# A mixer block on one core: first block normalised by ln and exp, polynomial sines on GpSimd, w2 in seven-row runs, fewer loads, another stored order

## The chip, the cores and the metric

One core of one Trainium2 chip. The metric is the device time of one execution in microseconds (us). Lower is better. The engines are named as in the profile: PE (TensorE matmuls), PEld (its weight loads), DVE (VectorE), ACT (ScalarE), POOL (GpSimd), SP (SyncE, here only the queue that issues most DMAs).

## The reference, cut to what matters

```python
xn = layernorm(x)                                   # x: [1, 2048, 448], bf16
# branch A: a diagonal complex recurrence of 448 states
Lam_bar = exp(exp(log_dt) * Lam);  B_bar = ((Lam_bar - 1) / Lam)[:, None] * B
h = Lam_bar * h + xn[t] @ B_bar.T                   # for each of 2048 steps t
s = 2 * real(h @ C.T) + xn * Dskip
# branch B: a gated MLP, F = 1792
y = layernorm(xn)
g = silu(gelu(y @ w1 + b1) @ w2 + b2)
out = x + s * g
```

The output is 2048 x 448 in bf16.

## The kernel before, in words

The 2048 rows are cut into four groups of 512 (`g` = 0 to 3), each into two blocks of 256 rows (`b`). A block lies on 128 partitions as two "parities" (`par`): partition p holds rows 2p and 2p+1. The work of a group is:

- `ln_stats`, `ln_scale`, `ln_apply` (lines 484 to 533): mean and variance by DVE, the reciprocal square roots for both layernorms by a chain of small operations, then two normalised copies, `xn_sb` for branch A and `xn2_sb` for branch B. For group 0 `ln_scale` is a chain of eleven dependent DVE operations on [128, 2 or 4] operands (an integer first guess and two Newton steps, lines 505 to 515). For later groups POOL or DVE does it.
- `xt` (line 535): transposes to `xnT` and `xn2T`. For `xn2T` of group 0 PE does them (line 544) and DVE copies the result from PSUM (line 550); all others are DMA transposes on the SP queue.
- `mm1` (line 768) and, for group 0, `mm1_half` (line 782): `w1` as stationary operand, `xn2T` as moving operand of 512 (or 256) columns, then GELU by ACT into `gT`. `mm1_half` does one block at a time, 7 steps of 8 matmuls for each block, into three pairs of PSUM banks in turn, so that the fourth step waits for the first step's GELU.
- `mm2` (line 799): 14 matmuls of `gT` by `w2`, then bias by DVE, tanh by ACT, gate by DVE.
- `bu` (line 703): B·x through `BT`, 14 or 7 matmuls of 256 columns into one PSUM bank, evacuated by ACT into `u_sb`.
- `ssm` (line 721): rotation by tables `WT`, DVE scans, rotation back into `h_sb`.
- `ym` (line 811): C·h plus the skip terms, times the gate, plus x, and the store.

The parameters are made once (`parameters`, line 558): four small vectors are loaded by the ACT queue, turned by PE (lines 561 to 565), and run through about forty operations on [128, 4] columns, nearly all on POOL (lines 572 to 621). The sine and cosine of two angles for each state come from two ACT `Sin` operations (lines 582 and 583). From the result come `lr`, `li` (real and imaginary part of Lam_bar), with which `lb` (line 666) makes a second copy of B, and the `BT` DMA transposes (line 674) follow; `cq` (line 685) makes `CQ` and `CZ` from the transposed C (`Cr`, line 678), and `m0` (line 693) a product of both. `tables` (line 628) makes the rotation tables `WT` by five ACT `Sin` operations after the last GELU of group 0.

PE first runs two batches of dummy matmuls on `ident` (line 858), 20 and 32 of them, with the turning of the parameters between them.

Three sets of ACT functions are in use (number 0 with exp and tanh, 9 with sin, 11 with GELU and tanh); where the next operation needs another set, the built program holds a load instruction for it (`ACT_TABLE_LOAD` in the trace). The program of the kernel before holds six.

The order of the instructions is not that of the text. Every operation is a `Task` with buffers read and written and an assumed duration, latency and priority; `Plan.order` (line 141) schedules them on a model of the five engines, `Plan.search` (line 220) changes priorities at random for 20,000 rounds, and `emit` (line 276) writes the best order out. Each engine runs its instructions strictly in that order and waits on semaphores. So every wait stands in front of all that follows on its engine.

Of the kernel before, what the change touches and what calls it, by code (L numbers as in the profile page):

```python
# [8 lines left out]
ACT = mybir.ActivationFunctionType  # L9
# [5 lines left out]
PINNED = -1e5  # L15

SLACK = 0.13
ENGS = ("pe", "act", "dve", "pool", "sp")

BEGIN, SWAP = 0.8, 1.28  # L20

AHEAD, AHEAD_T = 5.5, 0.9

HEAT = 0.03

DRAIN = 0.1

FULL = (0, 0)


class Task:

    __slots__ = ("eng", "ins", "reads", "writes", "dur", "lat", "prio", "sem", "nbytes", "idx",
                 "deps", "succ", "start", "end", "name", "chain", "alts", "alt", "table", "far", "mode", "move", "hold")

    def __init__(self, eng, ins, reads, writes, dur, lat, prio, sem, nbytes, name):
        self.eng, self.ins, self.reads, self.writes = eng, ins, tuple(reads), tuple(writes)  # L40
        self.dur, self.lat, self.prio, self.sem, self.nbytes = dur, lat, prio, sem, nbytes
        self.name = name
        self.deps, self.succ = set(), []
        self.start = self.end = None
        self.chain = False
        self.table = self.mode = None
        self.far, self.move, self.hold = AHEAD, 0.0, 0.0
        self.alts, self.alt = [(self.eng, self.ins, self.dur, self.lat)], 0

    def choose(self, k):  # L50
        self.alt = k
        self.eng, self.ins, self.dur, self.lat = self.alts[k]
        if self.sem in ENGS:
            self.sem = self.eng


class Plan:
# [3 lines left out]
    GBPS = 285.0  # L61
# [21 lines left out]
    def add(self, eng, ins, reads=(), writes=(), dur=0.2, lat=0.1, prio=0.0, sem=None, nbytes=0, name="",  # L83
            chain=False, table=None):
        if callable(ins):
            ins = [ins]
        t = Task(eng, ins, reads, writes, dur, lat, prio, sem or eng, nbytes, name)
        t.idx = len(self.tasks)
        t.chain = chain
        t.table = table  # L90
        self.tasks.append(t)
        return t

    def either(self, first, second, reads=(), writes=(), prio=0.0, chain=False):

        t = self.add(first[0], first[1], reads, writes, dur=first[2], lat=first[3], prio=prio)
        t.alts.append((second[0], second[1] if isinstance(second[1], list) else [second[1]], second[2], second[3]))
        t.chain = chain
        return t

    def dma(self, eng, out_ap, in_ap, reads=(), writes=(), prio=0.0, nbytes=0, transpose=False, dur=0.45, name="dma"):
        sem = f"d{self.ndma}"
        self.ndma += 1
        self._sem(sem)

        def fn(e):
            if transpose:
                return e.dma_start_transpose(out_ap, in_ap)
            return e.dma_start(out_ap, in_ap)  # L109
        if transpose:  # L110
            dur = 1.3
        if eng == "pool":
            dur = 1.0
        t = self.add(eng, fn, reads, writes, dur=dur, lat=1.4 if transpose else 1.8, prio=prio, sem=sem, nbytes=nbytes, name=name)
        t.far = AHEAD_T if transpose else AHEAD
        t.move = 1.3 * nbytes / 229376 if transpose else nbytes / (self.GBPS * 1e3)
        return t

    def link(self):
# [17 lines left out]
        for t in self.tasks:  # L137
            for d in t.deps:
                d.succ.append(t)

    def order(self):
        left = {t: len(t.deps) for t in self.tasks}
        ready = {e: [] for e in ENGS}
        free = {e: BEGIN for e in ENGS}
        table, mode = None, 0
        dma_free = 0.0
        at = {}
        pick = {e: None for e in ENGS}
        out = []

        def enter(t):
            m = t.hold
            for d in t.deps:
                end = d.end - d.lat + 0.03 if d.sem == t.eng else d.end + 0.03
                if end > m:
                    m = end
            at[t] = m
            ready[t.eng].append(t)

        for t in self.tasks:  # L160
            if not left[t]:
                enter(t)
        stale = set(ENGS)
        while True:
            for e in stale:
                r = ready[e]
                if not r:
                    pick[e] = None
                    continue
                f = free[e]  # L170
                first = min([at[t] for t in r])
                limit = (first if first > f else f) + SLACK
                best = None
                for t in r:
                    if at[t] <= limit and (best is None or t.prio < best.prio or (t.prio == best.prio and t.idx < best.idx)):
                        best = t
                pick[e] = (first if first > f else f, best)
            stale.clear()
            e = None
            for k in ENGS:  # L180
                if pick[k] is not None and (e is None or pick[k][0] < pick[e][0]):
                    e = k
            if e is None:
                break
            t = pick[e][1]
            start = max(at[t], free[e])
            if t.table and t.table != table:
                start = max(at[t], free[e] + SWAP)
                table = t.table
            if e == "pe":  # L190
                if (t.mode or FULL)[0] != mode:
                    start += DRAIN
                mode = (t.mode or FULL)[1]
            t.start = start
            done = start + t.dur
            t.end = done + t.lat
            if t.nbytes:
                if e == "sp":
                    done = max(done, dma_free + t.move - t.far)
                begin = start + (0.2 if t.far == AHEAD_T else t.dur)  # L200
                if t.nbytes > 8192 and begin < dma_free:
                    begin = dma_free
                t.end = begin + t.move + t.lat
                if t.nbytes > 8192:
                    dma_free = t.end - t.lat
            free[e] = done
            ready[e].remove(t)
            stale.add(e)
            for u in t.succ:
                left[u] -= 1  # L210
                if not left[u]:
                    enter(u)
                    stale.add(u.eng)
            out.append(t)
        assert len(out) == len(self.tasks)
        self.total = max(t.end for t in out)
        out.sort(key=lambda t: (t.start, t.idx))
        return out

    def search(self, rounds, seed=1):  # L220


        tail = {}
        for t in reversed(self.tasks):
            tail[t] = t.dur + max([tail[s] + (t.lat if s.eng != t.eng else 0.03) for s in t.succ], default=0)
        given = [t.prio for t in self.tasks]
        both = [i for i, t in enumerate(self.tasks) if len(t.alts) > 1]

        loads = [i for i, t in enumerate(self.tasks) if t.nbytes > 8192 and given[i] > PINNED]

        def run(prios, alts, holds):
            for t, p, a, h in zip(self.tasks, prios, alts, holds):
                t.prio = p
                t.hold = h
                if a != t.alt:
                    t.choose(a)
            self.order()
            return self.total

        alts, holds = [t.alt for t in self.tasks], [t.hold for t in self.tasks]  # L240
        free = [i for i, p in enumerate(given) if p > PINNED]
        now = None
        for alpha in (0.0, 0.1, 0.3, 1.0, 3.0, 1000.0):
            prios = [p - alpha * tail[t] if p > PINNED else p for t, p in zip(self.tasks, given)]
            total = run(prios, alts, holds)
            if now is None or total < now:
                now, here = total, (prios, alts, holds)
        best, keep = now, here
        mean = sum(here[0][i] for i in free) / len(free)
        scale = math.sqrt(sum((here[0][i] - mean) ** 2 for i in free) / len(free))  # L250
        rng = random.Random(seed)
        for r in range(rounds):
            prios, alts, holds = list(here[0]), list(here[1]), list(here[2])
            n = rng.choice((1, 1, 2, 4, 8))
# [7 lines left out]
            elif kind < 0.6:  # L262
                i, d = rng.randrange(len(free)), rng.gauss(0, scale * rng.choice((0.02, 0.1, 0.3)))
                for j in free[i:i + n]:
                    prios[j] += d
# [675 lines left out]
```

## Time and profile before

| | |
|---|---|
| median of 4 runs | 165.27 us (164.82 to 166.33) |
| the profiled execution | 165.44 us, of which 163.70 us are the span of the profile |
| busy, share of the span | PE 96%, DVE 77%, ACT 57%, POOL 17% |
| first `mm1_half` matmul | 10.43 us |
| start of the last matmuls, of the last DVE operation | 160.03 us, 160.79 us |
| one `ACT_TABLE_LOAD` | 1.28 us, six in all |
| matmuls | 993 |

The page gives one profiled execution. Its chain of waits follows the last instruction back to what released each step; the timeline lists the instructions in order of time with the idle time in front of them and what ended it. A matmul's record is longer than the distance to the next one, since matmuls are pipelined; the chain and the distances between the starts tell what a stream of them costs.

### The profile page before, as it was taken

The page shows a single profiled execution, that of the slowest core. Times are in us where ns is not written, and L with a number is a line of the kernel's source. Part 1 is how long each engine was busy: PE and PEld are TensorE (multiplying, and loading weights), DVE is VectorE, ACT ScalarE, POOL GpSimd, SP SyncE. Part 2 cuts the span into 40 slices and gives each one's busy share as a digit, 9 for nine tenths or more (in the row PEclk, how much of TensorE's full clock was granted, in tenths as well). Part 3 has the DMA queues.
Part 4 walks back from the last instruction along what each step waited for, and adds up shares of the span by engine and source line. Part 5 has one row for each costly group of instructions (what it writes and reads, how often), then busy time and mean ns, then how long its engine had stood idle before and what let it go on. Part 6 is the DMA issues. An engine that isn't in the chain of part 4 may idle for free.

```text
span 163.7 us, 2764 instructions
## 1 busy us (share of the span) xinstructions
PE 157.0 (96%) x993; PEld 95.4 (58%) x993; DVE 126.0 (77%) x264; ACT 92.9 (57%) x151; POOL 28.1 (17%) x96
## 2 busy tenths in 40 slices
PE   5979999999999999999999999999999999999991
PEld 5958985656546665554445455666566655555561
DVE  4866999657979989998989973545983699988563
ACT  3756984996868898627729544221449672541100
POOL 5866000700000030000606550000005020000000
PEclk9999999999999999999999999999999999999999
DMA  4999999798777000920000047440201000100111
GB/s 123 275 282 305 334 168 171 146 179 155 165 163 234 0 0 0 72 60 0 0 0 2 4 112 152 93 103 9 56 0 56 0 4 0 56 0 0 60 56 58
DMA packets 32807, 14.95 MB, mean 91 GB/s; under 512 B 25973, under 2 KB 32761, under 8 KB 32794
## 3 DMA queue, kind: packets, MB, share of 16 engines
q1 hardware_dynamic: 32738, 14.66, 40.6%
q0 software_dynamic: 48, 0.11, 0.3%
q8 instruction: 8, 0.13, 0.3%
q14 instruction: 5, 0.04, 0.1%
q10 hardware_dynamic: 8, 0.00, 0.0%
HBM read 7.00 MB, written 1.84 MB: 54 GB/s over the span
## 4 chain that ended last, share of the span: by engine, by line
PE 92%; DVE 2%; ACT 2%; DMA 1%; ACTq 1%; issue 0%
PE psum L803 24%; PE psum L772 22%; PE psum L707 13%; PE psum L824 12%; PE psum L788 9%; PE psum L827 4%; PE psum L696 3%; PE psum L858 2%; DMA vrows<-in_A_Dskip_dram 1%; ACT WT L647 1%; PE psum L544 1%; PE psum L833 1%; DVE t L837 1%; ACTq L109 1%; DVE tmp L839 1%
## 5 line engine op out<-in xcount | busy, mean ns | idle before, releaser
L803 PE MATMUL psum<-w_sb,gT 128*128 128x448 bf16 x224 | 44.7, 352 | 0.0
L772 PE MATMUL psum<-xn2T,w_sb 128*128 128x512 bf16 x168 | 38.7, 379 | 0.1
L803 PEld LDWEIGHTS psum<-w_sb,gT 128*128 128x128 bf16 x224 | 21.7, 98 | 18.6
L779 ACT ACTIVATE gT<-psum 128x1024 bf16<-128x1024 f32 x21 | 21.5, 1024 | 17.5 <-PE psum L772 17.1
L772 PEld LDWEIGHTS psum<-xn2T,w_sb 128*128 128x128 bf16 x168 | 16.2, 98 | 17.6 <-issue 0.3
L707 PE MATMUL psum<-xnT,BT 128*128 128x256 bf16 x196 | 24.0, 272 | 0.3 <-ACT WT L647 0.3
L707 PEld LDWEIGHTS psum<-xnT,BT 128*128 128x128 bf16 x196 | 19.0, 98 | 5.7 <-ACT WT L647 0.7
L807 ACT ACTIVATE th<-o 128x448 f32<-128x448 f32 x16 | 9.1, 575 | 22.8 <-DVE o L806 22.7
L806 DVE TENSOR_TENSOR o<-psum,b2bc 128x448 f32<-128x448 f32 x16 | 9.9, 621 | 9.2 <-PE psum L803 9.2
L788 PE MATMUL psum<-xn2T,w_sb 128*128 128x256 bf16 x112 | 14.4, 294 | 0.8 <-DVE xn2T L550 0.8
L837 DVE TENSOR_TENSOR t<-psum,g_sb 128x448 bf16<-128x448 f32 (+2 forms) x17 | 10.1, 595 | 6.4 <-PE psum L827 4.8
L732 DVE TENSOR_TENSOR_SCAN s_f<-cw,cur,v_sb 128x256 f32<-128x256 f32 x21 | 14.5, 735 | 0.2
L788 PEld LDWEIGHTS psum<-xn2T,w_sb 128*128 128x128 bf16 x112 | 11.7, 105 | 3.3 <-DVE xn2T L550 1.1
L808 DVE SCALAR_TENSOR_TENSOR g_sb<-th,o 128x448 bf16<-128x448 f32 x16 | 9.8, 619 | 3.0 <-ACT th L807 2.8
L824 PE MATMUL psum<-CQ,h_sb 128*128 128x448 bf16 (+2 forms) x63 | 12.0, 332 | 0.0
L824 PE MATMUL psum<-CZ,h_sb 128*128 128x448 bf16 x56 | 11.9, 352 | 0.0
L795 ACT ACTIVATE gT<-psum 128x512 bf16<-128x512 f32 x14 | 8.2, 595 | 6.4 <-PE psum L788 6.1
L746 POOL TENSOR_TENSOR cwk<-s_f,ang 128x3 f32<-128x3 f32 x3 | 1.2, 409 | 58.0 <-DVE s_f L732 58.0
L711 ACT ACTIVATE u_sb<-psum 128x512 bf16<-128x512 f32 x12 | 7.1, 595 | 6.8 <-PE psum L707 6.2
L488 DVE BATCH_NORM_STATS2 lnst<-x_all 128x6 f32<-128x448 bf16 x16 | 9.7, 614 | 1.3 <-DMA x_all<-in_A_x_dram 1.2
L528 DVE TENSOR_SCALAR xn_sb<-x_all,lnw 128x448 bf16<-128x448 bf16 x21 | 7.9, 394 | 2.1 <-ACT xn_sb L529 1.1
L529 ACT ACTIVATE xn_sb<-x_all,lnw 128x448 bf16<-128x448 bf16 x11 | 7.9, 750 | 2.1 <-DVE xn_sb L528 2.1
(130 smaller groups left out, 195.3 us busy)
## 6 DMA issues: line engine op xcount, KB each, us to landing
w_sb<-in_B_w_dram SPq DMA_DIRECT2D x2, 784.0 KB, 10.2
out_dram<-tmp SPq DMA_DIRECT2D x7, 224.0 KB, 1.9
w_sb<-in_B_w_dram SPq DMA_DIRECT2D x2, 672.0 KB, 7.0
x_all<-in_A_x_dram SPq DMA_DIRECT2D x3, 448.0 KB, 5.0
x_all<-in_A_x_dram SPq DMA_DIRECT2D x2, 224.0 KB, 2.7
gT<-in_A_C_re_dram SPq DMA_DIRECT2D x1, 392.0 KB, 9.9
Bn<-in_A_B_re_dram SPq DMA_DIRECT2D x1, 336.0 KB, 8.5
Bn<-in_A_B_im_dram SPq DMA_DIRECT2D x1, 336.0 KB, 8.1
```

The costliest lines, as they stand in the source:

```text
L488: dve([lambda e, b=b, par=par, q=q: e.bn_stats(lnst[:, q, :], x_all[:, 2 * g + b, par, :])], [f"x{2 * g + b}"] + (["xmT0_0"] if (g, b, par ...
L707: fns = [lambda e, r=r, m=m, d=d: e.matmul(psum[:, 4, r * NK:(r + 1) * NK], BT[:, m, d, :], xnT[:, gx, d, :], start=(d == 0), stop=(d == 6 ...
L732: dve(lambda e, i=i, ri=ri, init=init: e.tensor_tensor_scan(s_f[:, i, ri, :], col(R2, i).to_broadcast([128, NK]), v_sb[:, i, ri, :], init, ...
L772: fns = [lambda e, k=k, d=d: e.matmul(psum[:, b0 + k, :], w1_sb[:, d, (2 * j + k) * 128:(2 * j + k + 1) * 128], rhs[:, d, :, :], start=(d ...
L779: act(lambda e: e.activation(gT[:, gb, 2 * j:2 * j + 2, :], psum[:, b0:b0 + 2, :], ACT.Gelu_apprx_tanh), [f"ps{b0}", f"ps{b0 + 1}"] + (WK ...
L788: fns = [lambda e, k=k, d=d: e.matmul(psum[:, banks[k], :].rearrange("p (r c) -> p r c", r=2)[:, :, cs], w1_sb[:, d, (2 * j + k) * 128:(2 ...
L803: fns = [lambda e, fi=fi: e.matmul(psum[:, bk, 0:D], gT[:, gb, fi, q * 128:(q + 1) * 128], w2_sb[:, fi, :], start=(fi == 0), stop=(fi == N ...
L806: dve(lambda e: e.tensor_tensor(o2[:, fb, :], psum[:, bk, 0:D], b2bc[:], ALU.add), [f"ps{bk}", "b2bc"], [f"oo{fb}"], 0.62, prio - 76)
L807: act(lambda e: e.activation(th[:, fb, :], o2[:, fb, :], ACT.Tanh, scale=0.5), [f"oo{fb}"] + (WK + WKP if g == 0 else []), [f"th{fb}"], 0. ...
L808: dve(lambda e: e.scalar_tensor_tensor(out=g_sb[:, gs, :], in0=th[:, fb, :], scalar=1.0, in1=o2[:, fb, :], op0=ALU.add, op1=ALU.mult), [f" ...
L824: fns = [lambda e, k=k: e.matmul(psum[:, bk, c0:c1], h_sb[:, hb, k, k0:k0 + 128], cm[:, k, c0:c1], start=(k == 0), stop=False) for k in ra ...
L837: dve(lambda e: e.tensor_tensor(t3[:, fb, c0:c1], psum[:, bk, c0:c1], g_sb[:, gs, c0:c1], ALU.mult), [f"ps{bk}", f"g{gs}"], [f"t3{fb}_{c0} ...
```

## The change

1. The first block of group 0 is normalised for each parity by itself. DVE takes mean and variance of one parity, ACT makes the reciprocal square root as exp(-0.5 ln(v)), DVE applies it, PE does four transposes and DVE a copy of 512 columns. The load of this block of x is in two halves. The scale of the branch-A copy of that block comes from a third Ln and Exp, and two POOL operations. Block 1 stays on the DVE chain. The first ACT operation, a warm-up, is Ln in place of Exp.
2. The two ACT `Sin` of the parameters are replaced by a polynomial on POOL: three operations to wrap the angle, one ACT `Abs`, ten POOL operations in a chain.
3. `w2` is loaded so that each partition reads seven neighbouring rows in one piece (7 x 448 elements); hidden feature 7p+t of a half then lies on partition p, and `w1`'s columns are taken with a step of seven elements (`fcol`) as the stationary operand of `mm1` and `mm1_half`.
4. Two loads of B (64 x 448 each) and two of C (112 x 4 x 64 each) are left out. The swapped copies that they made are replaced by taking the two halves of the partitions crosswise in `combine`, two operations of 64 partitions in place of one of 128, for the last tile of each of B, CQ and CZ.
5. The load of block 1 of x is moved behind the first half of `w1`. The dummy matmuls are 28 and 8. The eight `De` and `Do` operations are made after the third GELU step.
6. The planner is taken out; a stored order takes its place, with `SECOND`, a list of the operations that go to their other engine.

```diff
-            act(lambda e: e.activation(sgn[0:1, 3:4], sgn[0:1, 2:3], ACT.Exp), ["sgn"], ["warm"], 0.2, S0, "exp")
+            act(lambda e: e.activation(sgn[0:1, 3:4], sgn[0:1, 2:3], ACT.Ln, scale=-1.0), ["sgn"], ["warm"], 0.2, 4 * PINNED, "exp")
...
-            ldx(0, 1, S1)
-            ldx(1, 1, S1)
+            for par in range(2):
+                ld("sp", x_all[:, 0, par, :], dram_ap(A_x, par * D, [[2 * D, 128], [1, D]]), [f"x0p{par}"], 114688, S1)
             ldw1(0, S1 + 1)
+            ldx(1, 1, S1 + 2)
...
-                for k, m in ((ri, 6), (1 - ri, 7)):
-                    ld("sp", Bn[k * 64:k * 64 + 64, m, D:896], dram_ap(bm, 384 * D, [[D, 64], [1, D]]),
-                       [f"Bn{m}{ri}"], 57000, S1 + 5, dur=0.55)
+                ld("sp", Bn[ri * 64:ri * 64 + 64, 6, D:896], dram_ap(bm, 384 * D, [[D, 64], [1, D]]), [f"Bn6{ri}"], 57000, S1 + 5, dur=0.55)
             for q in range(2):
                 ld("sp", w2_sb[:, q * 7:q * 7 + 7, :],
-                   dram_ap(B_w2, q * 7 * 128 * D, [[D, 128], [128 * D, 7], [1, D]]), [f"w2_{q}"], 803000, S1 + 6, dur=1.7)
+                   dram_ap(B_w2, q * 7 * 128 * D, [[7 * D, 128], [D, 7], [1, D]]), [f"w2_{q}"], 650000, S1 + 6, dur=1.7)
...
-                    for a, n, o in (((0, D, 0), (384, 64, 960)), ((0, 384, 512), (384, 64, 448), (384, 64, 896)))[ri]:
+                    for a, n, o in (((0, D, 0),), ((0, 384, 512), (384, 64, 448)))[ri]:
...
+            def first_norm():
+                for par in range(2):
+                    q = 2 * par
+                    var, mean = lnmv[:, 0, q, 1:2], lnmv[:, 0, q, 0:1]
+                    r1 = lnw[:, 0, 2, 1, q:q + 1]
+                    src, dst = x_all[:, 0, par, :], xn2_sb[:, 0, par * 512:par * 512 + D]
+                    dve(lambda e, q=q, src=src: e.bn_stats(lnst[:, q, :], src), [f"x0p{par}"], [f"st{q}"], 0.62, 2 * PINNED + par)
+                    dve(lambda e, q=q: e.bn_aggr(lnmv[:, 0, q, :], lnst[:, q, :]), [f"st{q}"], [f"mv0_{q}"], 0.16, 2 * PINNED + par)
+                    kb.add("act", [lambda e, var=var, r1=r1: e.activation(r1, var, ACT.Ln, scale=1.0 + LN_EPS, bias=eps[:, 1:2]),
+                                   lambda e, r1=r1: e.activation(r1, r1, ACT.Exp, scale=-0.5)], [f"mv0_{q}", "eps", "warm"], [f"r1{par}"],
+                           dur=0.5, lat=0.2, prio=4 * PINNED, chain=True, table="exp")
+                    dve(lambda e, src=src, dst=dst, mean=mean, r1=r1: e.tensor_scalar(dst, src, mean, r1, op0=ALU.subtract, op1=ALU.mult),
+                        [f"x0p{par}", f"r1{par}", f"mv0_{q}", "xm0"], [f"xm0p{par}"], 0.4, 2 * PINNED + par + 0.5)
+                    bank, oap = 6 - par, xn2T[:, 0, par * 4:par * 4 + 4, 0:128]
+                    pe([lambda e, d=d, par=par, bank=bank: e.transpose(psh[:, bank, d * 128:(d + 1) * 128], xn2_sb[:, 0, par * 512 + d * 128:par * 512 + d * 128 + 128],
+                                                                       ident[:, :]) for d in range(4)], [f"xm0p{par}", "ident"], [f"ps{bank}"], 0.33, 2 * PINNED)
+                    dve(lambda e, bank=bank, oap=oap: e.tensor_copy(oap, psh[:, bank, 0:512].rearrange("p (d c) -> p d c", d=4)), [f"ps{bank}"], [f"xmT0p{par}"], 0.42, 2 * PINNED + 2)
+                r0, n0, var = lnw[:, 0, 2, 0, 0:4:2], lnw[:, 0, 3, 0, 0:4:2], lnmv[:, 0, 0:4:2, 1]
+                kb.add("act", [lambda e: e.activation(r0, var, ACT.Ln, bias=eps[:, 0:1]), lambda e: e.activation(r0, r0, ACT.Exp, scale=-0.5)],
+                       ["mv0_0", "mv0_2", "eps", "r10", "r11"], ["r0"], dur=0.5, lat=0.2, prio=3 * PINNED, chain=True, table="exp")
+                kb.add("pool", [lambda e: e.tensor_tensor(n0, lnmv[:, 0, 0:4:2, 0], r0, ALU.mult), lambda e: e.tensor_scalar(n0, n0, -1.0, None, op0=ALU.mult)],
+                       ["mv0_0", "mv0_2", "r0"], ["lnw0_0"], dur=0.6, lat=0.15, prio=S0 + 2, chain=True)
...
-                act(lambda e: e.activation(ang[:, 2, :, :], ang[:, 1, :, :], ACT.Sin, scale=TWO_PI), ["an", "am", "cr"], ["as"], 0.25, 3 * PINNED, "sin")
-                act(lambda e: e.activation(ang[:, 3, :, :], ang[:, 3, :, :], ACT.Sin, scale=-TWO_PI, bias=sgn[:, 3:4]), ["am", "sgn3", "cr"], ["ac"], 0.3, 3 * PINNED + 1, "sin")
...
+                kb.add("pool", wrap, ["f1", "f3", "f4"], ["f1"], dur=0.24 * len(wrap), lat=0.15, prio=A2, chain=True)
+                act(lambda e: e.activation(YB, YA, ACT.Abs), ["f1", "f2"], ["f1"], 0.2, 3 * PINNED + 2)
+                kb.add("pool", sine, ["f1"], ["as", "ac"], dur=0.24 * len(sine), lat=0.15, prio=A2, chain=True)
...
+                ps = [(slice(0, 128), slice(0, 128), cb)]
+                if isinstance(cb, tuple):
+                    ps = [(slice(0, 64), slice(64, 128), cb[0]), (slice(64, 128), slice(0, 64), cb[1])]
...
+            def fcol(fi):
+                q, t = divmod(fi, 7)
+                return slice(q * 896 + t, q * 896 + 896, 7)
...
-                fns = [lambda e, k=k, d=d: e.matmul(psum[:, b0 + k, :], w1_sb[:, d, (2 * j + k) * 128:(2 * j + k + 1) * 128],
+                fns = [lambda e, k=k, d=d: e.matmul(psum[:, b0 + k, :], w1_sb[:, d, fcol(2 * j + k)],
...
-            for n, each, rd, pri in ((20, 0.107, [], 2 * PINNED), (32, 0.06, ["ps7"], 2 * PINNED + 1)):
+            for n, each, rd, pri in ((28, 0.1, [], 2 * PINNED), (8, 0.06, ["ps7"], 2 * PINNED + 1)):
...
-            kb.emit(20000, 2)
+            kb.emit()
```

The order of the instructions on each engine, as the built programs have it, at the places that the prediction speaks of:

```
ACT after:   load set 5, Ln (warm-up) | Ln, load set 0, Exp (parity 0) | load set 5, Ln, load set 0, Exp (parity 1)
             | copy of the turned parameters, Exp, dcol | load set 5, Ln, load set 0, Exp (branch A) | Exp | load set 11
             | GELU, Abs, GELU x2, Do, GELU, xn, GELU, xn, GELU x2, De, GELU x4, Abs of the table, GELU x3 | load set 9, Sin ...
PE before:   40 mm1_half, 8 transposes, 64 mm1_half, mm2, 8 mm1_half, mm2, bu, mm2, bu, ...
PE after:    40 mm1_half, 8 transposes, 72 mm1_half, mm2 x3, bu, mm2, bu, mm1, bu, ...
POOL after:  ... angle (5 operations), scale of branch A (2), den, f2, wrap (3), 2 of den, sine (10), lr, ..., li, ...
SP after:    x block 0 in two halves, w1 (3 loads), x block 1, w1, B (4), w2 (2), x, C re, C im, xnT, xnT, C im,
             BT x4, xn2T x2, BT x3, xnT x2, Cr x4, ...
```

## The prediction

> **What bounds the kernel now.** I read the page first. Its table of busy times says that PE is the bound:
>
> ```profile
> PE 157.0 (96%) x993; PEld 95.4 (58%) x993; DVE 126.0 (77%) x264; ACT 92.9 (57%) x151; POOL 28.1 (17%) x96
> ```
>
> PE's work is the same after the change but for 16 dummies, so a gain must come from time in which PE has nothing useful to do. The chain of waits, in order of time, shows where that is (start, duration, what):
>
> ```profile
> 4.95 3.61 PE psum L858 x32
> 8.61 1.05 PE psum L544 x8
> 9.68 0.70 DVE xn2T L550
> 10.43 6.19 PE psum L788 x40
> 16.62 0.45 PE psum L544 x8
> 17.06 6.99 PE psum L788 x64
> ...
> 30.22 1.66 PE psum L707 x14
> 31.90 0.60 ACT u_sb L711
> 32.50 1.04 ACT WT L647
> 33.56 0.52 ACT WT L647
> 34.10 0.52 ACT WT L647
> 34.78 1.69 PE psum L707 x14
> 36.46 2.65 PE psum L803 x14
> ```
>
> Useful PE work begins at 10.43. From there it hardly stops: the detour by ACT at 31.90 hides 14 L803 matmuls (the timeline has them at 31.70, and they take 2.65), so PE idled only from 34.35 to 34.78, 0.43 us. The table by stretches (length, then busy time of PE, PEld, DVE, ACT, POOL, then granted clock, DMA share, GB/s) has PE full from there on:
>
> ```profile
> 10.43:36.46 26.03, 25.77 (x191) 19.05 (x192) 20.98 (x56) 19.29 (x31) 7.03 (x24) 1.00 1.09 223
> 36.46:158.78 122.32, 122.25 (x718) 68.42 (x716) 96.41 (x179) 66.79 (x106) 14.20 (x38) 1.00 0.24 53
> ```
>
>  In distances between starts, the rest is: 112 matmuls L788 at 0.109 = 12.2, transposes 0.45, 21 L772 steps at 1.73 = 36.3, 16 L803 at 2.65 = 42.4, 196 L707 at 0.109 = 21.4, eight L824 with L827 at 2.08 = 16.6, eight with L833 at 1.52 = 12.2, four L696 at 1.38 = 5.5: 147.1 us. PE took 149.8 (10.43 to 160.28). The 2.7 left are 0.43 of stall, 0.5 of small ones, and a slow beginning: the list of L788 has records of two sizes,
>
> ```profile
> L788 PEld LDWEIGHTS psum<-xn2T,w_sb x112: 97/98/151, 10.4 to 27.2; 128*128 128x128 bf16 x112
> L788 PE MATMUL psum<-xn2T,w_sb x112: 272/273/421, 10.4 to 27.3; 128*128 128x256 bf16 x112
> ```
>
> and the first two steps of 8 end 1.68 us apart (GELU at 12.35 and 14.03), the later ones 0.87: about 16 matmuls at half rate, 16 x 0.105 = 1.7 us (the granted-clock column says 1.00 all the same). So the change can win at the start (before 10.43), and at most 2.7 behind it.
>
> The start is decided by ACT, as the timeline of ACT lets one price (start, duration, operation):
>
> ```profile
> 7.34 0.21 ACT L580 ACTIVATE cw<-cw 128x4 f32<-128x4 f32 x1
> 7.57 1.28 ACT L582 ACT_TABLE_LOAD   x1
> 8.86 0.21 ACT L582 ACTIVATE ang<-ang 128x8 f32<-128x8 f32 x1
> 8.97 0.29 ACT L583 ACTIVATE ang<-ang,sgn 128x8 f32<-128x8 f32 x1
> 9.28 1.28 ACT L795 ACT_TABLE_LOAD   x1
> ```
>
> A small ACT operation takes 0.2, a table load 1.28, back to back. The loads stand where the built program has them, and the program after has ten, not six: Ln is taken from set 5 and Exp from set 0, so each pair costs a load in between.
>
> **Part by part. The first block.** Removed: the DVE chain of eleven operations (4.81 to 6.81, 2.0 us). Now: x's first half (112 KB in place of 224). The whole block landed 2.6 us after its issue at 0.79; a store of 112 KB took 1.7. Between 2.5 and 3.4 I take 3.0. Mean and variance: 0.62 + 0.16, so ACT's Ln starts at 3.9 (its warm-up ends at 3.65). Then in one queue: Ln 0.2, load 1.28, Exp 0.2 (to 5.6); load, Ln (7.1); load, Exp of parity 1 (8.6). DVE applies in 0.4 (9.1), four transposes take 0.6 (three at 0.13 and the pipeline's 0.3: 9.8), the copy of half as many columns 0.4 against 0.69, hand-overs 0.05 each: PE starts L788's work at 10.3. Against 10.43: **-0.1** (ends -0.4 and +0.3 from the landing). The first half of w1 is there (issue 1.71, landing 6.1 to 7.0 later).
>
> *Table loads, page and trace.* The Trainium skill, "ScalarE: Activation LUTs", section "Table sets: the hidden batching unit", says that ln and then exp need one load, since one set has both. By it the five loads from Exp of parity 0 to that of branch A fall away, and the sum would be that of the first rival below, 162.4, instead of 165.0. The built order contradicts it and decides. The same page puts a switch at 2.66 us with a drain; this trace has 1.28 and the next operation 0.01 later.
>
> **ACT behind it.** Parameter copy, Exp, dcol (0.6, to 9.25), load, Ln, load, Exp (12.25), Exp (12.47), load: the first GELU starts at 13.8 where it was 12.35. The fourth step of PE needs that GELU's bank: if PE is at half rate at first, as before, the fourth step is due at 14.7, after the GELU's end at 14.35, and nothing is lost. If PE is at full rate (dummies and turning now run without a break from 1.9 to 6.4; before, they had one at 3.74 to 4.32), PE waits for ACT, and of the 1.7 only some 0.35 come through. Half of that: **-0.15**.
>
> **The sines.** Two ACT operations and two loads go; ten dependent POOL operations come. POOL's dependent ones stand 0.31 apart (starts 5.53, 5.82, 6.13). POOL's queue now has the branch-A scale in front of the wrap, waiting for Exp at 12.25; then 2 x 0.31, 2 x 0.2, 3 x 0.31 to 14.2, Abs behind the first GELU to 14.5, 2 x 0.2 more, ten to 17.8, `lr` 18.0, `li` 18.9, its negative 19.5. Before, `lr` was made at 9.15. Who waits: DVE, with `lb`'s first product, queued behind the copy of block 1 (17.85). DVE loses 1.1 to 1.6 us there, and everything on DVE is queued behind it: rest of the table 4.5, stats 2.75, so the second LB is done at 28.5.
>
> **The cover.** PE after the start: 14.5 us of L788 and transposes (10.43 to 24.92 without the L803 in between) to 24.8, three L803 to 32.75, then bu. The SP queue: xnT at 25 (DVE's last copy), C, BT 27 to 28.3, BT 28.5 to 29.8, landing 3.2 after issue at 31.7: bu is covered by 1.0. Two BT to 32.8, xn2T (DVE's copies after POOL's 3.1 us scale) 33.5 to 36.1, landing 38.0 against PE's 38.4; the next two BT to 38.7, landing 40.6 against 40.15. So **+0.45**, and the rotation tables, on ACT by 30.4 with u_sb free for bu at 34.3, no longer stall PE: **-0.43**. The bounds of the new stall: 0 if POOL keeps 0.25, and +2.5 if POOL's spacing is the 0.36 that its last three show (14.03, 14.31, 14.75: 16 x 0.1 = 1.6 more) and DVE makes none of it good.
>
> **Loads.** w2 in long runs: SP needs 2.9 us for its two issues; w1's halves, with fewer pieces, 0.5 each. Two loads of B (0.6 each) and two of C (0.58 each, at 36.78 and 38.69 among the transposes) go. All this is SP time; PE meets none of it at the start (w2 landed by about 20, needed at 24.05), and the C loads are already out of my SP sums. Three combines cost a second half-operation, 0.45 on DVE twice and 0.66 on ACT: DVE is idle 23%, and CQ's last product is due some 2 us before its use. 0. Dummies, x block 1 later (its chain starts at 10.3, ends at 15, transposes due at 16.5): 0.
>
> **w1 by steps of seven.** No row has a strided weight load. A load's record is 98 at full rate and 151 at half: 53 ns scale, 45 do not. So it occupies 53 ns, below the 109 of L788 and the 216 of L772: doubled, it stays hidden (0); from 2.3 times on, L788 slows by over 1.65 us in all; at four times (212) 112 x 0.103 = 11.5. Below nothing it cannot go, being hidden. I take 0, nearest to the row as it is.
>
> *Stride, page and trace.* The Trainium skill, "SBUF — State Buffer", section "Door 1: The DMA port swizzle", speaks of 16-byte lines with two hits wanted on each, and of eight bf16 as the free stride. Seven are 14 bytes: free by the stride, nearly a line for each column by the hits. By the one the sum stays 165.0, by the other it grows by an amount that the page does not give. No run here shows it yet.
>
> **The sum.** -0.1 - 0.15 - 0.43 + 0.45 = -0.23. The profiled execution took 165.44 (span 163.70 and 1.74 around), so 165.2; it lies 0.17 over the median, so the median would be **165.0**.
>
> **Rivals.**
> - *The loads don't cost.* If Ln and Exp ran with one set, PE would start after the dummies (6.4), eight transposes and a copy, at 8.0: -2.4, and -0.43: 165.27 - 2.83 = 162.4. For: the rewrite's own cost of 0.5 for a pair. Against: ten loads in the program, and six out of six appeared in the trace.
> - *Strided weights (slower).* Place: each of the 112 L788 matmuls. Deciding from 2.3 times the load's 53 ns; at three times 112 x 0.05 = 5.6, 170.6; at four 176.5. Against: the cover of 56 ns.
> - *Parameters too late (slower).* POOL at 0.36, DVE full in that stretch (20.98 of 26.03 us busy before): bu, mm1 and the Cr transposes late by 2.5 in place of 0.45: 167.1.
> - *The new order.* The 0.5 of small stalls go and PE is at full rate early: 164.2; part of my forecast's own range, 163.9 to 166.5.
>
> **Chances.** Forecast 0.62, loads free 0.10, strided 0.14, parameters late 0.14. 1%, 1.65 us, is about what a measurement of this kernel can tell from none. Faster by more (below 163.6): loads free 0.10 and 0.04 of the forecast: 0.14. Slower (over 166.9): strided 0.13, parameters 0.08, forecast 0.04: 0.25. Same: 0.61. The range reaches to the free loads and past the late parameters: 162.4 to 168.0, leaving out most of the strided case (0.12) and tails (0.06).
>
> **What would show it.** First L788 at 10.3, with four ACT_TABLE_LOAD in front of it and the GELU at 13.8: right; at 8, the loads are free. L788's loads at 98, spacing 0.109: strides free. `lr` on POOL at 18, DVE idle at 18 to 19.5, a PE wait before the third pair of bu: the late parameters. The forecast falls if PE starts before 9.5, if L788 stands over 124 ns apart, or if PE idles over 2 us between 25 and 50.

## The result and the profile after

| | before | after |
|---|---|---|
| median | 165.49 us (71 runs, 163.94 to 166.96) | 165.47 us (45 runs, 165.22 to 166.05) |
| the profiled execution | 165.44, span 163.70 | 165.45, span 163.7 |
| first `mm1_half` matmul | 10.43 us | 10.28 us |
| first GELU | 12.35 us | 13.60 us |
| matmuls | 993 | 977 |

The ratio of the times is 1.0002, with a 95% interval of 0.9991 to 1.0014. The change makes no difference that can be measured; 165.0 had been forecast (from a median before of 165.27 in four runs), and "same" with 0.61. The medians agree, but the parts do not: two gains of the prediction came, one came by half, its loss did not come where it was put, and another came that it did not have.

The page's table of busy times after has PE still as the bound, less busy by the 16 dummies and the gaps at the start:

```profile
PE 154.4 (94%) x977; PEld 99.6 (61%) x977; DVE 124.5 (76%) x251; ACT 98.9 (60%) x156; POOL 33.7 (21%) x115
```

The chain of waits after, in order of time (start, duration, what), no longer goes back to PE at 4.95. It runs on ACT through table loads (the lines without a tile), then on POOL through the sine, through one copy on DVE, and reaches PE only at 18.95:

```profile
7.20 1.28 ACT L369
...
9.09 1.28 ACT L378
10.38 0.30 ACT lnw L378
10.70 1.28 ACT L378
...
12.28 0.20 POOL lnw L380
...
13.23 0.30 POOL ang L468
...
17.45 0.23 POOL ang L477
17.75 0.37 POOL cw L487 x2
18.32 0.59 DVE xn2T L438
18.95 6.32 PE psum L694 x56
25.27 7.95 PE psum L709 x42
33.22 1.53 PE psum L608 x14
34.75 2.65 PE psum L709 x14
37.40 1.53 PE psum L608 x14
```

The last lines show the removed stall: the mm2 (L709) ends at 37.40, and the second pair of bu (L608) starts there. Before, PE stood idle at this place, from 34.35 to 34.78, waiting for the rotation tables. The timeline of PE shows what came in its place (idle time and its releaser at the end of a line):

```profile
9.19 0.54 PE L374 MATMUL psum<-ident,xn_sb 128*128 128x128 bf16 x4 [2.64 <-DVE xn_sb L371]
10.28 3.96 PE L694 MATMUL psum<-xn2T,w_sb 128*128 128x256 bf16 x24 [0.56 <-issue]
14.45 1.93 PE L694 MATMUL psum<-xn2T,w_sb 128*128 128x256 bf16 x16 [0.21 <-ACT ang L480]
16.22 0.61 PE L432 MATMUL psum<-ident,xn_sb 128*128 128x128 bf16 x8
16.66 1.91 PE L694 MATMUL psum<-xn2T,w_sb 128*128 128x256 bf16 x16
18.95 6.32 PE L694 MATMUL psum<-xn2T,w_sb 128*128 128x256 bf16 x56 [0.38 <-DVE xn2T L438]
```

Of the first half-group's matmuls, the first 24 take 3.96 us, at a lowered clock as the stretches show further down; then PE waits for ACT; and at 18.95 it waits for block 1's copy. In this list 0.38 of that wait is idle time, but the earlier records end with their pipeline: by starts, 16 matmuls from 16.66 at 0.109 end their share at 18.41, so the wait costs 0.54.

The timeline of DVE at that place gives the reason. The copy L438 is ready to run when the transposes end (16.8), but the reciprocal L499 stands ahead of it in DVE's queue and waits for POOL's parameters:

```profile
15.91 0.39 DVE L416 TENSOR_SCALAR xn_sb<-x_all,lnw 128x448 bf16<-128x448 bf16 x1
18.14 0.18 DVE L499 RECIPROCAL cw<-cw 128x4 f32<-128x4 f32 x1 [1.84 <-POOL cw L487]
18.23 0.66 DVE L438 COPY xn2T<-psum 128x1024 bf16<-128x1024 bf16 x1
```

**The balance, before to after, by starts on PE.** The first matmul is 0.15 earlier. At block 1's transposes the lead is 0.23 (16.45 against 16.22). The copy behind the reciprocal costs 0.54, and all of `mm1_half` is done at 25.27, where it would have been at 24.92 before, its interleaved mm2 taken out (24.05 + 0.87): 0.35 late. The stall that is gone turns this into a lead of 0.03 at the second pair of bu (34.78 against 37.40, which has one mm2 of 2.65 more in front of it). At PE's last matmul the lead is 0.22 (160.03 against 159.81); which part gained the 0.19 on the way was not traced. DVE's last operation, behind it, starts 0.02 earlier (160.79, 160.77). So the last 0.2 are lost on DVE's closing operations: 0.07 where after has a DMA issue on DVE's queue (159.22) that before does not have there, the rest between them, which no run here took apart.

### The profile page after: what moved, and what is told of

It reads as the page before. It is cut to its first block, busy times and chain, and to the rows that moved or that the text cites. A ratio compares the mean times of both kernels' runs of the same rounds, so it can differ in the third digit from the quotient of the medians.

```text
span 163.7 us, 2747 instructions
## 1 busy us (share of the span) xinstructions
PE 154.4 (94%) x977; PEld 99.6 (61%) x977; DVE 124.5 (76%) x251; ACT 98.9 (60%) x156; POOL 33.7 (21%) x115
## 4 chain that ended last, share of the span: by engine, by line
PE 85%; ACT 5%; POOL 3%; DVE 2%; DMA 1%; issue 1%; DVEq 0%
PE psum L709 26%; PE psum L678 22%; PE psum L608 13%; PE psum L730 12%; PE psum L694 4%; PE psum L733 4%; PE psum L597 3%; ACT L378 2%; ACT L369 2%; DMA x_all<-in_A_x_dram 1%; PE psum L739 1%; DVE t L743 1%; ACT L368 1%; DVE tmp L745 1%; POOL cw L487 1%
## 5 line engine op out<-in xcount | busy, mean ns | idle before, releaser
L709 PE MATMUL psum<-w_sb,gT 128*128 128x448 bf16 x224 | 44.2, 352 | 0.0
L709 PEld LDWEIGHTS psum<-w_sb,gT 128*128 128x128 bf16 x224 | 21.8, 98 | 19.3
L678 PEld LDWEIGHTS psum<-xn2T,w_sb 128*128 128x128 bf16 x168 | 21.6, 132 | 12.5 <-issue 0.2
L608 PE MATMUL psum<-xnT,BT 128*128 128x256 bf16 x196 | 24.0, 273 | 0.0
L608 PEld LDWEIGHTS psum<-xnT,BT 128*128 128x128 bf16 x196 | 19.0, 98 | 4.8 <-issue 0.4
L694 PEld LDWEIGHTS psum<-xn2T,w_sb 128*128 128x128 bf16 x112 | 12.6, 134 | 2.5 <-issue 1.2
L417 ACT ACTIVATE xn_sb<-x_all,lnw 128x448 bf16<-128x448 bf16 x16 | 11.4, 749 | 0.1
L730 PEld LDWEIGHTS psum<-CQ,h_sb 128*128 128x128 bf16 x63 | 6.0, 98 | 4.2
L352 DVE BATCH_NORM_STATS2 lnst<-x_all 128x6 f32<-128x448 bf16 x14 | 8.3, 603 | 0.0
L730 PEld LDWEIGHTS psum<-CZ,h_sb 128*128 128x128 bf16 x56 | 5.4, 98 | 4.6
```

The source lines that it names most:

```text
L417: ("act", lambda e: e.activation(dst, src, ACT.Identity, bias=nb, scale=rs), 0.75, 0.2)]
L608: fns = [lambda e, r=r, m=m, d=d: e.matmul(psum[:, 4, r * NK:(r + 1) * NK], BT[:, m, d, :], xnT[:, gx, d, :], start=(d == 0), stop=(d == 6 ...
L678: fns = [lambda e, k=k, d=d: e.matmul(psum[:, b0 + k, :], w1_sb[:, d, fcol(2 * j + k)], rhs[:, d, :, :], start=(d == 0), stop=(d == 3)) fo ...
L694: fns = [lambda e, k=k, d=d: e.matmul(psum[:, banks[k], :].rearrange("p (r c) -> p r c", r=2)[:, :, cs], w1_sb[:, d, fcol(2 * j + k)], rhs ...
L709: fns = [lambda e, fi=fi: e.matmul(psum[:, bk, 0:D], gT[:, gb, fi, q * 128:(q + 1) * 128], w2_sb[:, fi, :], start=(fi == 0), stop=(fi == N ...
L730: fns = [lambda e, k=k: e.matmul(psum[:, bk, c0:c1], h_sb[:, hb, k, k0:k0 + 128], cm[:, k, c0:c1], start=(k == 0), stop=False) for k in ra ...
```

## The experiments

Each was timed beside the kernel before on the same chip; the ratios are to that, and differences to after are taken from its median, 165.47. The kernel before had medians of 165.16, 165.40 and 165.69 in the three batches of runs, so differences worked out from the ratios come out up to 0.7 us away from these. Line numbers shift between the kernels; the names of the tiles do not.

### One table set for Ln and Exp

```diff
+# ahead of the warm-up Ln on ACT, put by hand: load of table set 6, which has ln and exp
+InstLoadActFuncSet(act_func_set_id=6)
```

> The kernel after, with one table load by hand of the set that holds both ln and exp (number 6) in front of the warm-up, so that the alternating loads fall away: 6 loads in all, 2 of them before the first GELU in place of 7. Theory (the loads in the ACT queue gave back what the rewrite of the first block won): the second parity's Ln starts right after its statistics at 5.7, its Exp ends at about 6.3, the first L694 matmul starts at 7.9 in place of 10.28, the first GELU at about 10, lr on POOL at 13 to 14 in place of 17.75; time 165.5 - 2.4 - 0.4 (the wait for the block-1 copy behind the reciprocal goes too) = 162.7. Rival (something else holds the start: the x halves, the dummies, w1's landing): the first matmul stays within 0.5 of 10.3 and the time within 165.0 to 165.9. Second rival (the start moves, but PE then waits later, for BT, xn2T or the tables): first matmul at 8, time 164.5 or more, with the difference seen as PE idle between 25 and 50.

Measured: **162.75 us**, ratio 0.9854 (0.9814 to 0.9895). ACT's Ln and Exp of both parities are done at 5.0, and the GELU's load is the next one. PE's timeline in this kernel:

```profile
7.26 2.80 PE L701 MATMUL psum<-xn2T,w_sb 128*128 128x256 bf16 x24 [0.70 <-DVE xn2T L383]
12.13 1.93 PE L701 MATMUL psum<-xn2T,w_sb 128*128 128x256 bf16 x16 [2.06 <-DMA w_sb<-in_B_w_dram]
13.89 0.61 PE L439 MATMUL psum<-ident,xn_sb 128*128 128x128 bf16 x8
14.34 8.02 PE L701 MATMUL psum<-xn2T,w_sb 128*128 128x256 bf16 x72
```

PE starts 3.0 earlier and the time falls by 2.7. A start that early meets the next thing that is late, the second half of w1 (2.06). POOL's sine ends five microseconds earlier too, so the copy of block 1 runs straight on and the 72 matmuls have no gap. What ate the rewrite's gain was the load between each Ln and each Exp.

### The loads batched instead

```diff
-Ln(p0) | load, Exp(p0) | load, Ln(p1) | load, Exp(p1) | ... | load, Ln(A) | load, Exp(A)
+Ln(p0), Ln(p1), Ln(A) | load, Exp(p0), Exp(p1), ..., Exp(A)
```

> The kernel after with ACT's operations of the first block reordered: all Ln first, one load, then all Exp: 3 loads up to the first GELU from the warm-up's on (sets 5, 0, 11) in place of 7. If the alternation of Ln and Exp is what holds the start, the first mm1 matmul is at 8.0 to 9.2 (10.28 in after), the first GELU at 9.5 to 10.5, and the time is 163.0 to 163.8, near the kernel with one table set (162.75), the remainder being parity 0, which now waits for parity 1's statistics. Rival, that each Ln costs a load by itself: start unchanged at about 10.3 and time 165.4.

Measured: **163.18 us**, ratio 0.9902 (0.9865 to 0.994). The first matmul is at 8.63, the first GELU at 10.55. So most of it is had without choosing a set by hand. The 0.4 between the two medians is less than their intervals can tell; what differs in the trace is that parity 0 waits for parity 1's statistics, and that PE's granted clock is 0.53 to 0.62 from 8 to 12. The alternation of Ln and Exp, not the operations, held the start.

### One load more

```diff
+# one more table load on ACT ahead of parity 1's Ln
```

> The kernel after, with one more table load (net) in front of parity 1's Ln. If ACT's queue of loads decides when PE starts and nothing behind hides it, the first L694 matmul (the half-group mm1) moves from 10.28 to about 11.6, the first GELU from 13.6 to 14.9, and the time from 165.47 by about +1.2 to 166.7 (ratio to before 1.007). Rival: the start is masked by what stands behind it (slow first steps, late GELU), then the first matmul still moves to 11.6, but the time stays within 165.3 to 166.0.

Measured: **166.93 us**, ratio 1.011 (1.0073 to 1.0148). The first matmul is at 11.67, the first GELU at 14.87. The time grew by 1.46, a little over the start's 1.39: a load more in that queue (1.28) is paid in full. In this kernel PE idles 4.07 before parity 1's transposes and has a granted clock of 0.50 until 16; the GELU is then no longer waited for, since PE is the slow one.

### The idle time filled with dummies

```diff
-            for n, each, rd, pri in ((28, 0.1, [], 2 * PINNED), (8, 0.06, ["ps7"], 2 * PINNED + 1)):
+            for n, each, rd, pri in ((28, 0.1, [], 2 * PINNED), (38, 0.06, ["ps7"], 2 * PINNED + 1)):
```

> The kernel after with 38 dummy matmuls in the second batch in place of 8, so that PE works on from 5.6 to about 8 instead of standing idle from 6.5 to 9.2. If the idle time is what lowers TensorE's granted clock (0.82, 0.50, 0.82 in 8 to 14 us of after), it stays near 1.00 there. The first GELU still starts at about 13.6, since ACT's table loads set it, so PE only waits longer for it: time 165.1 to 165.6, no difference that can be measured. Rival, that the slow clock at the start did reach the end: 0.6 to 1.2 less, 164.3 to 164.9. Slower, if the dummies hold up parity 0's transposes past the reciprocal square root of parity 1 (8.9 us): up to +0.4.

Measured: **165.38 us**, ratio 0.9985 (0.9962 to 1.0008), against after's 1.0002. The table by stretches shows the clock (length, busy time of PE, PEld, DVE, ACT, POOL, granted clock, DMA share, GB/s), first for after:

```profile
8.00:10.00 2.00, 0.54 (x4) 0.27 (x4) 0.97 (x3) 1.94 (x6) 0.98 (x5) 0.82 1.04 241
10.00:12.00 2.00, 1.72 (x9) 1.29 (x10) 1.89 (x7) 1.96 (x4) 0.19 (x1) 0.50 1.04 294
12.00:14.00 2.00, 2.00 (x17) 1.80 (x15) 1.70 (x9) 1.97 (x4) 1.39 (x7) 0.82 1.14 315
```

and for the kernel with 38 dummies:

```profile
8.00:10.00 2.00, 0.54 (x7) 0.23 (x4) 1.06 (x3) 1.94 (x6) 0.94 (x5) 1.00 1.05 335
10.00:12.00 2.00, 1.81 (x17) 1.84 (x18) 1.86 (x8) 1.97 (x3) 0.23 (x1) 1.00 1.12 281
12.00:14.00 2.00, 1.00 (x10) 0.75 (x7) 1.69 (x10) 1.96 (x5) 1.43 (x6) 1.00 1.10 354
```

PE's timeline in this kernel says where the speed went:

```profile
10.19 2.81 PE L694 MATMUL psum<-xn2T,w_sb 128*128 128x256 bf16 x24 [0.56 <-issue]
14.50 1.93 PE L694 MATMUL psum<-xn2T,w_sb 128*128 128x256 bf16 x16 [1.50 <-ACT gT L701]
```

The 24 matmuls take 2.81 in place of 3.96, and PE then waits 1.50 for the GELU in place of 0.21. The next 16 start at 14.50 against 14.45. Filling this idle time keeps the clock at 1.00, and the late GELU hides the gain whole.

### The reciprocal behind the copy

```diff
# stored order: task 59 (reciprocal of the parameters, DVE) moved from before task 105
# (copy of block 1's transposes, DVE) to right behind it
```

> The kernel after, with the DVE reciprocal of the parameters moved in DVE's order from in front of the copy of block 1's transposes to behind it. In the trace of after the reciprocal waited for POOL until 18.14 and the copy stood behind it (18.23), and PE waited for the copy until 18.95. Theory (this wait costs PE 0.4 to 0.6): copy at 17.0 to 17.6, no PE wait at 18.9, time 165.5 - 0.5 = 165.0. Rival (PE is paced by ACT's late GELUs there anyway): 165.5, the wait of PE then shows as one for ACT.

Measured: 165.23 us, ratio 1.001 (0.9985 to 1.0036). The wait is gone from PE's timeline:

```profile
16.21 0.61 PE L417 MATMUL psum<-ident,xn_sb 128*128 128x128 bf16 x8
16.66 8.02 PE L679 MATMUL psum<-xn2T,w_sb 128*128 128x256 bf16 x72
24.52 2.81 PE L694 MATMUL psum<-w_sb,gT 128*128 128x448 bf16 x14
```

mm2 starts at 24.68 by the chain, in place of 25.27. That shows what the copy waited for. In time it is inconclusive: the traced execution, 164.67, was the fastest of twelve, and the medians differ by 0.24, less than the interval.

### The polynomial taken out

```diff
-                kb.add("pool", sine, ["f1"], ["as", "ac"], dur=0.24 * len(sine), lat=0.15, prio=A2, chain=True)
+                act(lambda e: e.activation(ang[:, 4, :, :, :], YB, ACT.Sin, scale=-TWO_PI, bias=sgn[:, 3:4]), ["f1", "sgn3"], ["as", "ac"], 0.3)
# the wrap on POOL ahead of the branch-A scale
```

> The kernel after with the ten polynomial operations on POOL replaced by one ACT Sin of all sixteen columns, right before the first GELU: one more table load on ACT, and the wrap goes ahead of the branch-A scale on POOL. If the polynomial's worth is ACT's time before the first GELU, that GELU moves from 13.6 to about 15.4, PE's fourth step waits for it about 1.8 longer, lr on POOL moves from 17.75 to about 14.5, and DVE's reciprocal no longer holds up block 1's copy (0.4 to 0.6 back): in all 166.5 to 167.0. Rival, that it bought nothing: 165.2 to 165.6.

Measured: **166.38 us**, ratio 1.0044 (1.0019 to 1.0069), 0.91 more than after. The timeline of ACT has one more load, and the GELU behind it:

```profile
12.41 1.28 ACT L466 ACT_TABLE_LOAD   x1
13.71 0.31 ACT L466 ACTIVATE ang<-ang,sgn 128x16 f32<-128x16 f32 x1
14.03 1.28 ACT L686 ACT_TABLE_LOAD   x1
15.32 1.57 ACT L686 ACTIVATE gT<-psum 128x512 bf16<-128x512 f32 x3
```

PE waits 1.73 for that GELU (0.21 in after), and the copy's 0.54 come back, since `lr` is made at 14.09 and the reciprocal no longer waits: 1.52 - 0.54 = 0.98, against 0.91 measured (0.7 by the ratios). mm2 starts at 26.08 in the timeline, 0.97 after the 25.11 of after. The polynomial is worth some 0.9 here, because it takes a load from ACT's queue ahead of the GELU; it cost the copy its 0.54.

### With one table set: B held back, and the polynomial again

```diff
# on top of the one table set: the four loads of B go behind the first block's second copy
+self.tasks[30].deps.add(self.tasks[94])
```

> The kernel with one table set (162.75 us), and the loads of B held back until the first block's second copy for xn2T is done. It tests why w1's second half lands at 12.0 there, 7.8 us after its issue, and lets PE wait for 2.1 us. If the loads of B share the DMA engines with it, it lands at about 9 to 10, the wait is gone, and the time is 160.7 to 161.5 unless B, w2 and C, later by some 3 us, stall PE afterwards. Rival, that its own size or something else than B sets the landing: wait unchanged, 162.7.

Measured: **162.52 us**, ratio 0.9866 (0.9813 to 0.992): the same as without. PE still waits for w1, now at two places:

```profile
8.19 2.80 PE L688 MATMUL psum<-xn2T,w_sb 128*128 128x256 bf16 x24 [1.02 <-DMA w_sb<-in_B_w_dram]
11.68 1.93 PE L688 MATMUL psum<-xn2T,w_sb 128*128 128x256 bf16 x16 [0.69 <-DMA w_sb<-in_B_w_dram]
```

The second half lands at 11.54 in place of 12.00. It was not at 9 to 10, so the theory fell in the form it had. But the test was weaker than it was meant to be: the loads of B are issued at 7.76 in place of 4.74, still well ahead of that landing, and over all the kernels the second half landed 6.8 to 8.4 us after its issue, so that 0.5 is within the spread. Whether w1's own size or the other loads on the busy DMA engines set the landing stays open.

On top of this kernel, the sine on ACT:

> The kernel before this one in the list (one table set, B held) with the ten polynomial operations on POOL replaced by one ACT Sin (two table loads' worth of ACT time, one more load of 1.28 between the last Exp and the first GELU). The polynomial's worth is that ACT goes to GELU sooner: the first GELU moves later by about 1.3 to 1.6, PE's fourth step waits for it by about that, and the time is 1.0 to 1.6 longer than that kernel's; lr on POOL moves 2.5 to 3 us earlier. Rival, that the polynomial bought nothing at this place: same time within 0.3 or less, since lr is earlier and the B copies with it.

Measured: 162.69 us, ratio 0.9863 (0.9823 to 0.9902). The rival holds, and for a reason that neither had: PE waits 1.74 for the GELU here, but where the polynomial stays it waits 1.71 (1.02 and 0.69) for w1 on the way to the same matmuls. The group of 16 starts at 12.14 in place of 11.68, 0.46 later. What was worth 0.9 in after is worth nothing that can be measured once another wait covers it.

### w1 in pieces of 128 columns, and by steps of 14

```diff
# contiguous, as before
-                return slice(q * 896 + t, q * 896 + 896, 7)
+                return slice(fi * 128, fi * 128 + 128)
# step 14
+                return slice(fi, fi + 1779, 14)
```

(w2's rows are loaded to match.)

> The kernel after with part 3 undone: w1's columns contiguous again, w2 loaded in pieces of one row. Theory (the longer weight loads, 132 ns in place of 98, are hidden behind matmuls of 109 and 216 ns): the weight loads' records back at 98, distances between matmuls unchanged, time 165.5 within 0.3. Rival (they cost PE part of what the start won): time lower by 0.5 to 1.5, L694 and L678 steps shorter than 0.87 and 1.73 us.

> The kernel after with the step doubled: hidden feature 14p+t on partition p, w1's columns by steps of 14 elements (28 bytes), w2 loaded so that each partition reads from one run of 14 rows in two halves of seven; both halves of w1 are waited for by every step. Theory (the load's price goes by the number of memory lines that it touches, and 7 elements already touch nearly one for each column): record 132 to 150, still hidden, time 165.5 within 0.4. Rival (the price goes with the step: +34 ns for 7, so +70 or more for 14): record 170 or more, occupation over the 109 ns of an L694 matmul, so L694 slows by 0 to 20 ns each, 112 x 0.02 = up to 2.2 us: 165.5 to 167.7.

Measured: contiguous **165.42 us**, ratio 1.0012 (0.9988 to 1.0035); step 14 **167.14 us**, ratio 1.0131 (1.0088 to 1.0173). Groups of weight loads (busy time, mean ns of one), contiguous:

```profile
L678 PEld LDWEIGHTS psum<-xn2T,w_sb 128*128 128x128 bf16 x168 | 16.2, 98 | 17.4 <-issue 0.2
```

step 7, that is, after:

```profile
L678 PEld LDWEIGHTS psum<-xn2T,w_sb 128*128 128x128 bf16 x168 | 21.6, 132 | 12.5 <-issue 0.2
```

and step 14:

```profile
L678 PEld LDWEIGHTS psum<-xn2T,w_sb 128*128 128x128 bf16 x168 | 22.8, 140 | 11.4 <-issue 0.2
```

98, 132 and 140 ns: a strided load is longer, but it grows little from 14 to 28 bytes of step, and the distance of the matmuls stays at 0.109 and a step of `mm1` at 1.73 in all three. The 1.7 us of step 14 need not come from the length of the weight loads: every step then reads columns of both halves of w1, and the first matmul waits until 11.51. The profile names a DVE operation in front of it, but the last piece of w1, issued at 4.2, landed 7.2 later, at 11.4. My edit changed a wait as well as the step, so its time says nothing on the stride; its records do.

## Why the prediction was right

**The start, -0.1.** It was -0.15. Every station was where the sum had put it: Exp of parity 1 done at 8.69 (8.6), first matmul 10.28 (10.3), first GELU 13.60 (13.8). The only wrong stone was x's second half, which landed at 4.85 where I had at most 3.4; ACT's loads hid that. That ACT's loads are the cause is shown from both sides: one more costs 1.46, those between Ln and Exp taken out give 2.7 (one set) or 2.3 (batched), by the medians.

**The half-rate clock, -0.15.** The step weighed two cases, slow PE with nothing lost and full rate with most of the 1.7 lost to the GELU. The slow one came, with a clock of 0.50, and by the transposes it had gained 0.08. The dummies showed the other, at the same time. The choice between the cases did not matter; I had priced their difference at about 0.35. And the slow case came by another way than "as before". Before, PE was at half rate from its first dummies on; in after it had reached full rate in the second batch, as one of the two cases supposed, and lost it in the idle time from 6.55 to 9.19, which the step did not weigh. The dummies tell the two rates (before, then the kernel with 38 dummies):

```profile
4.95 3.59 PE L858 MATMUL psum<-ident 128*128 128x128 bf16 x32
5.56 2.36 PE L764 MATMUL psum<-ident 128*128 128x128 bf16 x38
```

**The sines.** `lr` came at 17.75 (18.0 forecast). The failed step is "Who waits": I let DVE wait with the first product of `lb`, *behind* block 1's copy. The reciprocal of the parameters waits too, and stands *ahead* of the copy, so PE lost 0.54 at 18.95. The order without its waits does not tell this; the tile that each of DVE's operations reads does.

**The cover, +0.45.** It did not come: the third pair of bu starts at 40.67, with no wait. The transfers were right: the `BT` transpose that the pair waits for was issued at 37.43 and landed 3.1 later, at 40.5 (40.6 forecast). PE was to be there at 40.15, and came 0.5 later because of the copy. So the loss was paid 20 us earlier, at nearly the same price; that the sum came out near is luck in these two terms, one priced at nothing and one that did not come. Nor would the stall have come back with the copy freed: with the reciprocal moved, the same transposes are issued 0.9 earlier and PE has no wait there at 39.90 either.

**The rotation tables, -0.43.** Right: no gap at 37.40, where the second pair of bu starts. All but the last of the tables' operations were done on ACT at 31.08 (30.4 forecast). Which part of the change removed the stall was not tested alone.

**The strided weights, 0.** Right in time (contiguous 165.42), by the cover that was named: the record grew by 34 ns, under the 56 ns that were free. I had taken the row as it is, 98, so the size was off. The Trainium skill, "SBUF — State Buffer", section "Door 1: The DMA port swizzle", was weighed in two readings, free by the stride or charged by the lines that are hit; the record is charged, at 14 bytes already, and the time is not.

**The rivals.** Loads that cost nothing: not as the program is built, but with the set chosen by hand the time is 162.75, near the 162.4 of that rival. There the Trainium skill's sentence on ln and exp sharing a set ("ScalarE: Activation LUTs", section "Table sets: the hidden batching unit") holds; the build had taken set 5 for the one and 0 for the other. Parameters too late: `lr` came no later than forecast, and the 2.5 us did not show. The new order: with 38 dummies PE is at full rate early, but the time is 165.38, not 164.2; the 0.5 of small stalls was not followed.

So the gain that the change could have had, some 2.7 us, went into five table loads between Ln and Exp, three of them ahead of the first matmul; and of what was left, 0.54 was given back at block 1's copy.

## What to carry to other kernels

When a chain on a slow engine is rewritten for ACT, count the table loads in the built order first: here three of them ahead of the first matmul, 1.28 us each, cost more than the whole chain that was replaced (2.0 us), and ordering the operations by function, or one load by hand, was worth 2.3 to 2.7 us by the medians. When a producer gets later, list every operation that reads it, not the one that one has in mind, and look at what stands behind each in its queue. An edit's worth is that of the wait it shortens: the same polynomial was worth 0.9 us with the GELU late, and nothing with w1 late at the same place.

## What the runs showed of the hardware

- TensorE's granted clock fell after some short idle times, and not after others. A gap of 2.64 us on PE (6.55 to 9.19 in after) was followed by 0.82, 0.50 and 0.82 in 8 to 14 us; one of 1.28 (batched loads) by 0.53 and 0.62 in 8 to 12; one of 1.09 (38 dummies) by 1.00. But the later gaps, behind the first 24 matmuls, left it at 1.00 though they were as long: 1.50 (38 dummies), 1.73 (polynomial taken out) and 2.06 (one table set, 10.07 to 12.13). So the length of the gap alone does not decide, and what does was not tested. The stretch behind the 2.06, with one table set:

```profile
12.00:14.00 2.00, 1.87 (x18) 1.89 (x19) 0.96 (x5) 0.78 (x2) 1.59 (x9) 1.00 1.08 337
```

- The Trainium skill, "TensorE: Matmul & The Clock Gate", section "What's actually happening", puts the return to half rate after an idle window of some 3.4 us; the gaps of 1.28 and 2.64 that were followed by a lower clock were shorter.
- In before the first two steps were slow as well, with the column at 1.00. PE had not been at full rate until then: its 32 dummies from 4.95 on took 3.59 us, against 2.36 for 38 in the kernel with 38 dummies. Why the column says 1.00 stays open.
- The kernel before spread over 3.0 us in 71 runs, after over 0.8 in 45. With the GELU late, PE's early pace no longer reaches the end, which would explain it. It fits the kernel with 38 dummies (0.5 in 12 runs) and the one with one table set and an early GELU (2.6 in 6 runs), but is not shown.
- The second half of w1 lands 6.8 to 8.4 us after its issue at the start of the program (4.20 to 12.00 with one table set), the first 4.5 to 6.3, with the DMA engines' share at about 1.0 from 4 us on; with one table set this is the next bound of the start.
